# Storing the last block of a fused attention and two-MoE kernel in two halves, with the chunks of its last matmul rounds reordered around them

## The chip, the cores and the metric

The kernel runs on one core of a Trainium2 chip. The metric is the device time of one execution in microseconds (us), the median of three runs.

## The reference

The inputs are q, k and v of shape (4, 12, 448, 64): 4 batches of 448 tokens, 12 heads of 64 columns. Attention is without a softmax, with a sigmoid per score; its output, 1792 tokens by 768 columns, goes through two mixture-of-experts layers, each with 8 experts of which every token takes one.

```python
scores = scale * q @ k.T - log(S)
attn = sigmoid(scores) @ v
x = attn.transpose(0, 2, 1, 3).reshape(B * S, H * D)
# first layer: tokens with x @ w_skip > 0 only
e = argmax(x @ w_gate); gate = max of softmax(x @ w_gate)
x = x + gate * (relu(x @ w1[e]) @ w2[e])
# second layer: all tokens, cosine router
e = argmax(xn @ en.T / tau); gate = max of softmax
out = gate * (relu(x @ v1[e]) @ v2[e])
```

## The kernel before

The time falls into three stages. **Attention** takes pairs of heads in steps `g`; a step is `score` (PE, into a `psS` tile), a sigmoid on ACT, and two steps later `av` (PE, into `psO`). The operands of the first pairs are turned by PE transposes in `turn_first(nm, i)`, for nm "k" and "q" and for the halves i = 0 and 1: PE writes a bank `ps_t`, and four copies bring it into the tiles `kT` and `qT` (the call's j = 0 on DVE at L589, j = 1 on ACT at L587). The operands of later pairs arrive by DMA (`load_qk` on SP's queue, `load_v` on ACT's) and are turned by DVE at L593. Small setup steps are put between the steps `g`; one of them, `emb_turn` (L167 on PE), needs the expert embeddings scaled by GpSimd (POOL, L127), and that scaling stands on DVE behind the turn of the third pairs' q.

**Each MoE layer** is done block by block (a block is one batch of 448 tokens): most tokens of a block go to one expert, and `dense` computes the block with that expert's weights. The hidden columns are cut into NF = 8 chunks f. `h(f)` is 18 matmuls of 448 columns into one of the two banks (L785 to L787, "bank<-xs"); ACT (L805) and DVE (L806) turn it into the high part `hh` and the low part `hl`; `y(f)` is 18 matmuls, three for each of six feature chunks c, into the accumulators `YS[0..5]` ("y<-hh"). PE's order is h(0), h(1), y(0), h(2), y(1) and so on. `sub(k)` is called once after each h and once after each y, k = 0 to 15, and runs what a table of steps puts there: the splits of the next weights (L775 on ACT, L776 on DVE), loads, routing.

**The few tokens of other experts** are an `Item`. In the last block of the second layer its steps stand in the table of that block: `select` (DVE, slot 0), then by the three numbers given to `schedule` the steps `places` (four small matmuls L926 on PE into a bank, out by DVE at L929), `gather` (64 times: POOL reads a token's number and copies its column, L938, into the tile `stg`) and `gate`; at slots 13 and 15 `h(0)` and `h(1)` (24 matmuls each, L961), whose transposes are `hT` (L974, copied by DVE to `sel` at L975), and at the end `y` (32 matmuls L985). `put` multiplies on DVE (L999) and writes the rows by an indirect DMA from POOL (L1000); it waits for the block's own stores, onto whose rows it writes.

**The end of a block** is `finish`: the six accumulators are copied to `STG` (even c on ACT at L1308, odd c on DVE at L1306), transposed 24 times on PE (L1320), multiplied by the gate into `ROW` (ACT L1316, DVE L1314) and stored to `out`. For the last block the store is in two pieces: the feature blocks 0 to 3 on SP's queue and 4 and 5 on ACT's (L1335). An engine runs its instructions in program order, and so does each queue.

Of the kernel before, what the change touches and what calls it, by code (L numbers as in the profile page):

```python
# [10 lines left out]
F32 = mybir.dt.float32  # L11
F32R = mybir.dt.float32r
I32 = mybir.dt.int32
AF = mybir.ActivationFunctionType
# [7 lines left out]
def sigmoid_attention_moe_moe_kernel(  # L22
# [19 lines left out]
    P = 112  # L42
# [486 lines left out]
    def attention():  # L529


        with ExitStack() as a:
# [39 lines left out]
            def turn_first(nm, i):  # L572
                if i == 0:
                    ST[0, nm] = wk.tile([128, 2, S], F32, tag=nm + "T", name=nm + "T")
                ps = bank("ps_t")
                for j in range(2):
                    for e in range(2):
                        nc.tensor.transpose(
                            ps[:, (2 * j + e) * P : (2 * j + e + 1) * P],
                            LDU[0][nm][:, i, j, 2 * e * D : (2 * e + 2) * D], ident[:P, :P],  # L580
                        )
                for j in range(2):
                    for o in range(2):
                        src = ps[D * o : D * o + D, 2 * j * P : (2 * j + 2) * P].rearrange("r (e p) -> r p e", e=2)
                        dst = ST[0, nm][D * j : D * j + D, i].rearrange("r (p e o) -> r p e o", e=2, o=2)[:, :, :, o]
                        if j:
                            nc.scalar.activation(dst, src, AF.Copy)  # L587
                        else:
                            nc.vector.tensor_copy(dst, src)  # L589
# [198 lines left out]

    NF = 2 * NU

    def dense(xs, sub, f0=0, f1=NF):

        def h(f):
            h1, l1 = W[f // 2 % 2][:2]
            g = f % 2 * 128
            ps = bank("ps_h")
            for c in range(ND):
                mm3(  # L800
                    ps[:, :S], h1[:, c, g : g + 128], l1[:, c, g : g + 128], xs[:, 0, c, :], xs[:, 1, c, :],
                    c == 0, c == ND - 1,
                )
            a, l = HH[f % 2], HL[f % 2]
            nc.scalar.activation(a, ps[:, :S], AF.Relu)  # L805
            nc.vector.scalar_tensor_tensor(l, ps[:, :S], 0.0, a.bitcast(F32), op0=ALU.max, op1=ALU.subtract)  # L806

        def y(f):
            h2, l2 = W[f // 2 % 2][2:]
            g = f % 2  # L810
            for c in range(ND):
                mm3(
                    YS[c][:, :S], h2[:, g, c * 128 : c * 128 + 128], l2[:, g, c * 128 : c * 128 + 128],
                    HH[f % 2], HL[f % 2], f == 0, f == NF - 1,
                )

        for f in range(f0, f1):
            h(f)
            sub(2 * f)
            if f:  # L820
                y(f - 1)
            sub(2 * f + 1)
        if f1 == NF:
            y(NF - 1)
# [42 lines left out]
    class Item:  # L867
# [99 lines left out]

            return f

        def hT(self, s):  # L970
            def f():
                ps = bank("ps_ht")
                for i in range(2):
                    nc.tensor.transpose(ps[:, i * 128 : i * 128 + 128], self.hs[:, i * 128 : i * 128 + 128], ident)  # L974
                nc.vector.tensor_copy(SEL[:, s * 256 : s * 256 + 256], ps[:, :256])  # L975

            return f
# [320 lines left out]
    e = expert_of(0)  # L1298
    b = nc.values_load(K["pb"][0:1, 8:9], engines=[ENG.SP], min_val=0, max_val=B - 1)

    def finish(j, b, end=False):

        for c in range(ND):
            o = STG[:, c * S : (c + 1) * S]
            if c % 2:
                nc.vector.tensor_copy(o, YS[c][:, :S])  # L1306
            else:
                nc.scalar.activation(o, YS[c][:, :S], AF.Copy)  # L1308
        g = dense_gate(R2, j)

        def scaled(c, d, n, t):
            row = ROW[:P, c * DM + d * 128 : c * DM + (d + n) * 128]
            if (c + (n == 2)) % 2:
                nc.vector.tensor_scalar(row, t, g[:, c : c + 1], None, op0=ALU.mult)  # L1314
            else:
                nc.scalar.activation(row, t, AF.Copy, scale=g[:, c : c + 1])  # L1316

        def turn(t, w, c, d):
            o = d * S + c * P
            nc.tensor.transpose(t[:P, w : w + 128], STG[:, o : o + P], ident)  # L1320

        def tail():
            if end:
                banks = BANKS + YS[1:5]
                for d0, n, m in ((0, 4, 1), (4, 2, 2)):
                    place = [(banks[d0 + c // m], c % m * 256) for c in range(C)]
                    for d in range(d0, d0 + n):
                        for c, (t, w) in enumerate(place):
                            turn(t, w + (d - d0) * 128, c, d)
                    for c, (t, w) in enumerate(place):  # L1330
                        scaled(c, d0, n, t[:P, w : w + n * 128])
                    cols = slice(d0 * 128, (d0 + n) * 128)
                    queue, bq = (nc.sync, b) if d0 == 0 else (nc.scalar, batch_of(j))
                    to = out.rearrange("(b c p) d -> p b c d", c=C, p=P)[:, ds(bq, 1), :, cols]
                    STORES.append(queue.dma_start(  # L1335
                        to.rearrange("p o c d -> p (o c) d"),
                        ROW[:P].rearrange("p (c d) -> p c d", d=DM)[:, :, cols],
                    ))
                tc.declare_no_dep(STORES[1].ins, STORES[0].ins, reason="disjoint columns")
                return  # L1340
            at = 0
            for c in range(C):
                for d0, n in ((0, 4), (4, 2)):
                    t = YS[at % ND]
                    at += 1
                    for d in range(d0, d0 + n):
                        turn(t, (d - d0) * 128, c, d)
                    scaled(c, d0, n, t[:P, : n * 128])
            nc.sync.dma_start(
                out.rearrange("(b c p) d -> p b c d", c=C, p=P)[:, ds(b, 1)].rearrange("p o c d -> p (o c) d"),  # L1350
                ROW[:P].rearrange("p (c d) -> p c d", d=DM),
            )

        return tail

    pend, STORES = None, []
    for j in range(B):
        box = {"e": e}
        last = j == B - 1
        if last:  # L1360
            todo = {}
        else:
            steps = route2_steps(j + 1, XST[(j + 1) % 2])
            todo = at_subs((3, 5, 7, 1, 2, 2, 5, 6, 8, 9, 11), steps)
        if j == 0:
            load_unit(v1, v2, e, 1)
            halves()
            for f in split_unit(0, FIRST_RAW)[3:]:
                f()
            todo = merge({-0.5: lambda: spread(item_b())}, todo)  # L1370
        if j == B - 2:
            todo = merge(todo, item_steps(R2, (11, 13, 15)))
        if pend:
            todo = merge({-0.5: pend}, todo)

        def units2(k):
            u, r = k // 4, k % 4
            if r == 0 and u + 2 < NU:
                load_unit(v1, v2, box["e"], u + 2)
            if k == 10 and not last:  # L1380
                box["n"] = expert_of(j + 1)
                load_unit(v1, v2, box["n"], 0)
            if (u + 1 < NU or not last) and r % 2 == 0:
                for f in split_unit((u + 1) % NU)[:3] if r == 0 else split_unit((u + 1) % NU)[3:]:
                    f()
            if k == 12 and not last:
                load_unit(v1, v2, box["n"], 1)

        xs = XST[j % 2]
        if not last:  # L1390
            dense(xs, beside(units2, todo))
            pend = finish(j, b)
            b, e = nc.values_load(K["pb"][0:1, 9 + j : 10 + j], engines=[ENG.SP], min_val=0, max_val=B - 1), box["n"]
            continue
        with tc.If(count(R2) > 0) as cmp:  # L1395
            it = Item(1, 0)
            at, prep = it.ready(0)
            dense(xs, beside(units2, schedule(merge(todo, at), prep, (3, 3, 7))))
            it.hT(1)()
            finish(j, b, True)()  # L1400
            it.finish([None] * 3)
            info = mybir.DependencyInfo(mybir.DependencyClass.Sync, mybir.DependencyReason.DATA)
            tc.add_manual_dep(it.put().ins, STORES[0].ins.name, info, reason="the rows it lands on")
        with cmp.Else():
            STORES = []
            dense(xs, beside(units2, todo))
            finish(j, b, True)()
    more = nc.values_load(R2.LI[0:1, 3 * NL + 1 : 3 * NL + 2], min_val=0, max_val=NL)  # L1408
    with tc.If(more > 0):
        others(1)  # L1410
# [33 lines left out]
```

## Time and profile before

| | |
|---|---|
| median of 3 runs | 579.96 us (579.85 to 580.21) |
| the profiled execution: its own time | 579.14 us |
| its span, first to last instruction | 577.3 us |
| PE busy | 557.1 us, 96% |
| DVE, ACT, POOL busy | 302.1, 262.9, 45.3 us |
| mean granted TensorE clock | 0.994 |

The own time of the profiled execution is 1.84 us more than its span, and 0.82 us less than the median. All times of the trace are counted from the start of the span.

### The profile page before, as it was taken

The page shows a single profiled execution, that of the slowest core. Times are in us where ns is not written, and L with a number is a line of the kernel's source. Part 1 is how long each engine was busy: PE and PEld are TensorE (multiplying, and loading weights), DVE is VectorE, ACT ScalarE, POOL GpSimd, SP SyncE. Part 2 cuts the span into 40 slices and gives each one's busy share as a digit, 9 for nine tenths or more (in the row PEclk, how much of TensorE's full clock was granted, in tenths as well). Part 3 has the DMA queues.
Part 4 walks back from the last instruction along what each step waited for, and adds up shares of the span by engine and source line. Part 5 has one row for each costly group of instructions (what it writes and reads, how often), then busy time and mean ns, then how long its engine had stood idle before and what let it go on. Part 6 is the DMA issues. An engine that isn't in the chain of part 4 may idle for free. (4 is left out here: it accounts for less than half of the span.)

```text
span 577.3 us, 10262 instructions
## 1 busy us (share of the span) xinstructions
PE 557.1 (96%) x3719; PEld 434.1 (75%) x3719; DVE 302.1 (52%) x766; ACT 262.9 (46%) x429; POOL 45.3 (8%) x147
## 2 busy tenths in 40 slices
PE   8999999999999999999999999999999999899994
PEld 4554645544599988998778999979997999799871
DVE  2634434256957678561368653687347664533021
ACT  5766766767832363430156333933266332422021
POOL 4010000000000000651000000000000000055100
PEclk9999999999999999999999999999999999999997
DMA  9999786876342414235563060713227060653343
GB/s 148 146 134 121 120 123 109 129 100 203 118 150 70 152 36 146 97 111 185 202 223 110 0 219 0 250 66 124 97 74 241 0 219 1 198 173 109 95 180 103
DMA packets 138206, 73.37 MB, mean 127 GB/s; under 512 B 102066, under 2 KB 128006, under 8 KB 138128
## 3 DMA queue, kind: packets, MB, share of 16 engines
q1 hardware_dynamic: 116384, 65.94, 43.4%
q10 hardware_dynamic: 21360, 5.97, 5.6%
q0 software_dynamic: 384, 0.53, 0.6%
q8 instruction: 36, 0.59, 0.5%
q14 instruction: 42, 0.34, 0.2%
HBM read 66.90 MB, written 5.70 MB: 126 GB/s over the span
## 5 line engine op out<-in xcount | busy, mean ns | idle before, releaser
L805 ACT ACTIVATE hh<-bank 128x448 fp32r<-128x448 f32 x48 | 26.0, 542 | 192.0 <-PE bank L787 165.8
L785 PE MATMUL bank<-xs,h 128*128 128x448 f32 x288 | 107.4, 373 | 3.2 <-DVE hl L806 1.3
L785 PE MATMUL y<-hh,h 128*128 128x448 f32 x288 | 107.5, 373 | 0.0
L786 PE MATMUL y<-hl,h 128*128 128x448 f32 x288 | 105.6, 367 | 0.0
L787 PE MATMUL y<-hh,l 128*128 128x448 f32 x288 | 105.6, 367 | 0.0
L786 PE MATMUL bank<-xs,h 128*128 128x448 f32 x288 | 105.3, 366 | 0.0
L787 PE MATMUL bank<-xs,l 128*128 128x448 f32 x288 | 105.2, 365 | 0.1
L606 ACT ACTIVATE A<-psS,bias 128x896 f32<-128x896 f32 x84 | 83.3, 1006 | 35.6 <-PE psS L602 35.3
L806 DVE SCALAR_TENSOR_TENSOR hl<-bank,hh 128x448 fp32r<-128x448 f32 x48 | 29.9, 623 | 123.2 <-ACT hh L805 122.2
L776 DVE TENSOR_TENSOR l<-r,h 128x512 fp32r<-128x512 f32 (+1 forms) x115 | 85.4, 792 | 4.6 <-ACT h L775 3.0
L602 PE MATMUL psS<-qT,kT 64*64 64x448 f32 x672 | 87.3, 541 | 0.3 <-ACT A L606 0.3
L620 PE MATMUL psO<-A,v 64*64 64x448 f32 x672 | 86.3, 539 | 0.0
L775 ACT ACTIVATE h<-r 128x512 fp32r<-128x512 f32 (+1 forms) x115 | 74.6, 710 | 0.0
L785 PEld LDWEIGHTS bank<-xs,h 128*128 128x128 f32 x288 | 54.0, 187 | 12.1 <-DVE hl L806 2.7
L620 PEld LDWEIGHTS psO<-A,v 64*64 64x64 f32 x672 | 34.7, 133 | 32.2 <-issue 19.9
L785 PEld LDWEIGHTS y<-hh,h 128*128 128x128 f32 x288 | 54.1, 188 | 6.0 <-issue 1.0
L787 PEld LDWEIGHTS bank<-xs,l 128*128 128x128 f32 x288 | 54.0, 188 | 5.4 <-DVE l L776 0.4
L787 PEld LDWEIGHTS y<-hh,l 128*128 128x128 f32 x288 | 54.1, 188 | 5.0
L786 PEld LDWEIGHTS y<-hl,h 128*128 128x128 f32 x288 | 54.1, 188 | 4.8 <-issue 0.2
L786 PEld LDWEIGHTS bank<-xs,h 128*128 128x128 f32 x288 | 54.1, 188 | 4.3
L602 PEld LDWEIGHTS psS<-qT,kT 64*64 64x64 f32 x672 | 32.5, 132 | 30.4 <-issue 16.2
L527 DVE COPY xT<-psO 64x448 f32<-64x448 f32 x24 | 14.9, 622 | 43.1 <-PE psO L620 42.9
(251 smaller groups left out, 451.8 us busy)
## 6 DMA issues: line engine op xcount, KB each, us to landing
r<-in_moe_w_dram SPq DMA_DIRECT2D x62, 768.0 KB, 6.0
k<-in_k_dram SPq DMA_DIRECT2D x44, 112.0 KB, 3.6
q<-in_q_dram SPq DMA_DIRECT2D x44, 112.0 KB, 4.8
v<-in_v_dram ACTq DMA_DIRECT2D x44, 112.0 KB, 3.7
out_dram<-row SPq DMA_DIRECT2D x3, 1344.0 KB, 6.8
out_dram<-row SPq DMA_DIRECT2D x1, 896.0 KB, 5.4
stg<-in_moe_w_dram SPq DMA_DIRECT2D x1, 768.0 KB, 6.5
row<-in_moe_w_dram SPq DMA_DIRECT2D x1, 768.0 KB, 7.7
```

The source lines that it names most:

```text
L527: nc.vector.tensor_copy(x, ps[64 * j : 64 * j + 64, :S])
L602: nc.tensor.matmul(ps[KT * i : KT * i + KT, j, :S], lhsT=kT[r, i, h * KT : (h + 1) * KT], rhs=qT[r, i], start=True, stop=True,)
L606: nc.scalar.activation(at, ps[:, :, :S], AF.Sigmoid, bias=bias, scale=1.0 / math.sqrt(D))
L620: nc.tensor.matmul(ST[w, "o"][i][D * j : D * j + D, :S], lhsT=t[r, j, h, :], rhs=at[r, j, :], start=h == 0, stop=h == NH - 1,)
L775: nc.scalar.activation(dst_h, src, AF.Copy)
L776: nc.vector.tensor_sub(dst_l, src, dst_h.bitcast(F32))
L785: nc.tensor.matmul(ps, lhsT=ah, rhs=bh, start=first, stop=False)
L786: nc.tensor.matmul(ps, lhsT=ah, rhs=bl, start=False, stop=False)
L787: nc.tensor.matmul(ps, lhsT=al, rhs=bh, start=False, stop=last)
L805: nc.scalar.activation(a, ps[:, :S], AF.Relu)
L806: nc.vector.scalar_tensor_tensor(l, ps[:, :S], 0.0, a.bitcast(F32), op0=ALU.max, op1=ALU.subtract)
```

## The change

Three things change.

1. In `turn_first` all four copies of k are done by DVE and all four of q by ACT (before: j = 0 of both by DVE, j = 1 by ACT), and the half i = 1 is written to a `psO` tile instead of the two banks.
2. In the last block the three numbers for the item's steps are (5, 5, 7) instead of (3, 3, 7): `places` and `gather` move from the slot behind y(0) to the slot behind y(1).
3. `dense` ends otherwise in the last block. Its last two rounds of y go chunk by chunk, each chunk is copied to `STG` as soon as it is complete, the feature blocks 0 to 2 are transposed and stored after chunk 3, and 3 to 5 after chunk 5. The item's h(1) stands now after three chunks of y(6), and its `hT(1)` behind the last chunk, in `YS[0]` instead of a bank. The number of the batch for ACT's store is read ahead of the chunks.

```diff
-                ps = bank("ps_t")
+                ps = psO.tile([128, 512], F32, tag="psO", name="ps_t") if i else bank("ps_t")
...
-                        if j:
+                        if nm == "q":
                             nc.scalar.activation(dst, src, AF.Copy)
...
             h(f)
             sub(2 * f)
+            if end and f == NF - 1:
+                end(yc, lambda: sub(2 * f + 1))
+                return
...
+    def finish_last(j, b, it=None):
+        place = {0: BANKS + YS[1:3], 3: YS[3:5] + BANKS}
...
+        def store(g, d0, queue, bq):
+            for c, t in enumerate(place[d0]):
+                scaled(g, c, d0, 3, t[:P, : 3 * 128])
...
+        def end(yc, rest):
+            g = dense_gate(R2, j)
+            bq = batch_of(j)
+
+            def both(c):
+                yc(NF - 2, c)
+                yc(NF - 1, c)
+                copy(c)
+
+            for c in range(3):
+                yc(NF - 2, c)
+            rest()
+            for c in range(3):
+                yc(NF - 1, c)
+                copy(c)
+            both(3)
+            for d in range(3):
+                turns(d)
+            store(g, 0, nc.sync, b)
+            both(4)
+            both(5)
+            turns(3)
+            turns(4)
+            if it:
+                it.hT(1, YS[0])()
+            turns(5)
+            store(g, 3, nc.scalar, bq)
...
-            dense(xs, beside(units2, schedule(merge(todo, at), prep, (3, 3, 7))))
-            it.hT(1)()
-            finish(j, b, True)()
+            steps = schedule(merge(todo, at), prep, (5, 5, 7))
+            dense(xs, beside(units2, steps), end=finish_last(j, b, it))
             it.finish([None] * 3)
```

The changed kernel's lines are some lower down: L1314 and L1316 become L1310 and L1312, L1306 and L1308 become L1352 and L1354, L929 becomes L935, L975 becomes L981.

At the very start of the program, ACT's rows before, from its first load to the first sigmoids:

```order
L544 DMA q_128<-in_q_dram 112x2x256 x2
L632 ACT_TABLE_LOAD
L632 ACTIVATE bias<-bias 128x1
L587 ACTIVATE kT<-ps_t 64x224 x2
L587 ACTIVATE qT<-ps_t 64x224 x2
L587 ACTIVATE kT<-ps_t 64x224 x2
L587 ACTIVATE qT<-ps_t 64x224 x2
L606 ACTIVATE A<-psS,bias 128x896 x3
```

and of the change:

```order
L544 DMA q_128<-in_q_dram 112x2x256 x2
L632 ACT_TABLE_LOAD
L632 ACTIVATE bias<-bias 128x1
L587 ACTIVATE qT<-ps_t 64x224 x8
L606 ACTIVATE A<-psS,bias 128x896 x3
```

ACT has eight copies in both; kT has left ACT, and on DVE qT has left in the same way.

In the last block, DVE's rows before, from the last step of `select` (sel) on. hl is the low part that L806 makes of an h, l are the weights' low parts, and L929 is the way out of `places`:

```order
L911 TENSOR_SCALAR sel<-io,small 112x128 x4
L806 SCALAR_TENSOR_TENSOR hl_78<-bank_1721,hh_76 128x448
L776 TENSOR_TENSOR l_1735<-r_92,h_1734 128x768 x2
L929 TENSOR_SCALAR stg<-bank_1721 1x64
L806 SCALAR_TENSOR_TENSOR hl_77<-bank_1720,hh_75 128x448
L776 TENSOR_TENSOR l_1729<-r_89,h_1728 128x512 x3
L806 SCALAR_TENSOR_TENSOR hl_78<-bank_1721,hh_76 128x448
```

and of the change:

```order
L917 TENSOR_SCALAR sel<-io,small 112x128 x4
L806 SCALAR_TENSOR_TENSOR hl_78<-bank_1721,hh_76 128x448
L776 TENSOR_TENSOR l_1735<-r_92,h_1734 128x768 x2
L806 SCALAR_TENSOR_TENSOR hl_77<-bank_1720,hh_75 128x448
L776 TENSOR_TENSOR l_1729<-r_89,h_1728 128x512 x3
L935 TENSOR_SCALAR stg<-bank_1720 1x64
L806 SCALAR_TENSOR_TENSOR hl_78<-bank_1721,hh_76 128x448
```

The way out of `places` stands one round later, behind the hl of h(2) and three splits, and its bank is that of h(2) (bank_1720) instead of that of h(1) (bank_1721).

At the end of the last block, DVE's rows before, from the copies of the two `hT` (sel; the first of them runs a round earlier) to `put`; y_1722 to y_1727 are the accumulators of the chunks 0 to 5 and later hold transposes, dg is the gate:

```order
L975 COPY sel<-bank_1720 128x256 x2
L1306 COPY stg<-y_1723 128x448
L1306 COPY stg<-y_1725 128x448
L1306 COPY stg<-y_1727 128x448
L347 TENSOR_TENSOR dgt<-OH_106,PRIM_110 112x32
L350 TENSOR_REDUCE dg<-dgt 112x4
L351 TENSOR_TENSOR dg<-dg,gr_363 112x4
L1314 TENSOR_SCALAR row<-bank_1721,dg 112x512
L1314 TENSOR_SCALAR row<-y_1724,dg 112x512
L1314 TENSOR_SCALAR row<-y_1725,dg 112x256
L1314 TENSOR_SCALAR row<-y_1726,dg 112x256
L999 TENSOR_SCALAR xg_73<-y_1722,small 128x384
```

and of the change (the rows of the gate, which now stand at the head, left out, as is `small` ahead of the last):

```order
L1352 COPY stg<-y_1723 128x448
L1352 COPY stg<-y_1725 128x448
L1310 TENSOR_SCALAR row<-bank_1721,dg 112x384
L1310 TENSOR_SCALAR row<-y_1724,dg 112x384
L1352 COPY stg<-y_1727 128x448
L981 COPY sel<-y_1722 128x256
L1310 TENSOR_SCALAR row<-y_1726,dg 112x384
L1310 TENSOR_SCALAR row<-bank_1721,dg 112x384
...
L1005 TENSOR_SCALAR xg_73<-y_1722,small 128x384
```

The copies of the accumulators stood behind the copy of `hT(1)` and now stand ahead of it, and half of the multiplications stands between them.

## Rows read from the trace of the kernel before

**Rows 1.** What POOL's queue ran for put, by line L1000; last columns first and last start.

```profile
L1000 POOLq EVENT_SEMAPHORE  x3: 43/43/43, 571.0 to 571.1; - x3
```

**Rows 2.** Timeline at the end: start us, us, engine, line, what [idle before <-releaser].

```profile
559.13 0.36 PE L787 MATMUL y<-hh,l 128*128 128x448 f32 x1
...
560.10 1.68 DVE L1306 COPY stg<-y 128x448 f32<-128x448 f32 x3
...
562.12 1.25 PE L1320 MATMUL y<-ident,stg 128*112 128x128 f32 x10
...
562.39 0.69 ACT L1316 ACTIVATE row<-bank,dg 112x512 f32<-112x512 f32 x1 [2.92 <-PE y L1320]
...
563.31 5.38 PE L985 MATMUL y<-r,sel 128*64 128x384 f32 x32
...
564.35 0.86 ACT L1316 ACTIVATE row<-y,dg 112x256 f32<-112x256 f32 x2 [0.69 <-DVE row L1314]
...
565.67 0.38 ACTq L1335 DMA_DIRECT2D out_dram<-row  x1
...
568.74 0.62 DVE L999 TENSOR_SCALAR xg<-y,small 128x384 f32<-128x384 f32 x1 [3.96 <-PE y L985]
```

**Rows 3.** DMA issues from 555 us on: KB each, us from issue to landing.

```profile
out_dram<-row SPq DMA_DIRECT2D x1, 896.0 KB, 5.4
out_dram<-row ACTq DMA_DIRECT2D x1, 448.0 KB, 5.3
```

**Rows 4.** Waits of PE in the last block: us in total, times, longest.

```profile
PE bank L926 <- DVE hl L806: 2.2, 1, 2.2
```

**Rows 5.** Timeline of PE in the last block, from y(0) to h(3).

```profile
501.41 0.37 PE L787 MATMUL y<-hh,l 128*128 128x448 f32 x1
503.96 0.61 PE L926 MATMUL bank<-sel,small 112*1 112x64 f32 x8 [2.18 <-DVE hl L806]
504.50 0.47 PE L785 MATMUL bank<-xs,h 128*128 128x448 f32 x1
...
511.91 0.37 PE L785 MATMUL bank<-xs,h 128*128 128x448 f32 x1
```

**Rows 6.** Timeline of DVE, POOL and PE, from hl to the item's h(0).

```profile
503.29 0.62 DVE L806 SCALAR_TENSOR_TENSOR hl<-bank,hh 128x448 fp32r<-128x448 f32 x1
...
505.56 0.20 DVE L929 TENSOR_SCALAR stg<-bank 1x64 int32<-1x64 f32 x1
...
506.37 0.20 POOL L938 COPY stg<-xT 128x6 f32 x1 [244.44 <-PE bank L787]
...
536.42 0.19 POOL L938 COPY stg<-xT 128x6 f32 x1 [0.27 <-issue]
...
542.38 2.81 PE L961 MATMUL bank<-r,stg 128*64 128x256 f32 x24
```

**Rows 7.** Timeline of DVE and POOL, one of four places where splits meet the gather.

```profile
517.14 1.83 DVE L776 TENSOR_TENSOR l<-r,h 128x768 fp32r<-128x768 f32 x2
...
517.36 2.07 POOL L938 COPY stg<-xT 128x6 f32 x5 [0.27 <-issue]
```

**Rows 8.** Timeline of the start, the copies of the first operands.

```profile
5.13 0.79 DVE L589 COPY kT<-ps_t 64x224 f32<-64x224 f32 x2 [1.80 <-PE ps_t L578]
...
6.02 0.73 ACT L587 ACTIVATE kT<-ps_t 64x224 f32<-64x224 f32 x2 [2.81 <-DVE kT L589]
...
6.80 0.60 PE L578 MATMUL ps_t<-ident,k 112*128 112x112 f32 x4 [0.78 <-ACT kT L587]
...
9.15 0.74 ACT L587 ACTIVATE qT<-ps_t 64x224 f32<-64x224 f32 x2
```

**Rows 9.** Timeline of DVE and PE, the turn ahead of the embeddings, and PE's wait for them.

```profile
28.18 1.11 DVE L593 STREAM_TRANSPOSE qT<-q 128x896 f32<-128x896 f32 x1 [1.31 <-DMA q<-in_q_dram]
...
32.95 0.53 PE L167 MATMUL ps_emb<-ident,emb 8*128 8x8 f32 x6 [0.77 <-POOL emb L127]
```

**Rows 10.** Windows: width, busy us of the engines, granted clock, DMA share, GB/s.

```profile
16.00:18.00 2.00, 2.00 (x28) 0.88 (x24) 0.70 (x1) 1.24 (x2) 0.00 (x0) 1.00 1.42 152
```

More of the change, by code (lines that the diff above doesn't have):

```diff
@@ L789, in sigmoid_attention_moe_moe_kernel, with dense @@
     NF = 2 * NU
-    def dense(xs, sub, f0=0, f1=NF):
+    def dense(xs, sub, f0=0, f1=NF, end=None):
         def h(f):
@@ L806, in h, with yc, y @@
             nc.vector.scalar_tensor_tensor(l, ps[:, :S], 0.0, a.bitcast(F32), op0=ALU.max, op1=ALU.subtract)
-        def y(f):
+        def yc(f, c):
             h2, l2 = W[f // 2 % 2][2:]
             g = f % 2
+            mm3(
+                YS[c][:, :S], h2[:, g, c * 128 : c * 128 + 128], l2[:, g, c * 128 : c * 128 + 128],
+                HH[f % 2], HL[f % 2], f == 0, f == NF - 1,
+            )
+        def y(f):
             for c in range(ND):
[L812 to L815, printed above, removed]
+                yc(f, c)
         for f in range(f0, f1):
@@ L968, in h, with hT @@
             return f
-        def hT(self, s):
+        def hT(self, s, at=None):
             def f():
-                ps = bank("ps_ht")
+                ps = bank("ps_ht") if at is None else at
                 for i in range(2):
@@ L1299, in sigmoid_attention_moe_moe_kernel, with scaled, turn_out, finish @@
     b = nc.values_load(K["pb"][0:1, 8:9], engines=[ENG.SP], min_val=0, max_val=B - 1)
-    def finish(j, b, end=False):
+    def scaled(g, c, d, n, t):
+        row = ROW[:P, c * DM + d * 128 : c * DM + (d + n) * 128]
+        if (c + (n == 2)) % 2:
+            nc.vector.tensor_scalar(row, t, g[:, c : c + 1], None, op0=ALU.mult)
+        else:
+            nc.scalar.activation(row, t, AF.Copy, scale=g[:, c : c + 1])
+    def turn_out(t, w, c, d):
+        o = d * S + c * P
+        nc.tensor.transpose(t[:P, w : w + 128], STG[:, o : o + P], ident)
+    def finish(j, b):
         for c in range(ND):
@@ L1309, in finish @@
         g = dense_gate(R2, j)
[L1311 to L1320, printed above, removed]
-        def tail():
[L1323 to L1340, printed above, removed]
+        def tail():
             at = 0
@@ L1346, in tail @@
                     for d in range(d0, d0 + n):
-                        turn(t, (d - d0) * 128, c, d)
-                    scaled(c, d0, n, t[:P, : n * 128])
+                        turn_out(t, (d - d0) * 128, c, d)
+                    scaled(g, c, d0, n, t[:P, : n * 128])
             nc.sync.dma_start(
@@ L1354, in finish, with copy, turns @@
         return tail
+    def finish_last(j, b, it=None):
+        place = {0: BANKS + YS[1:3], 3: YS[3:5] + BANKS}
+        def copy(c):
+            o = STG[:, c * S : (c + 1) * S]
+            if c % 2:
+                nc.vector.tensor_copy(o, YS[c][:, :S])
+            else:
+                nc.scalar.activation(o, YS[c][:, :S], AF.Copy)
+        def turns(d):
+            d0 = d // 3 * 3
+            for c, t in enumerate(place[d0]):
+                turn_out(t, (d - d0) * 128, c, d)
+        def store(g, d0, queue, bq):
+            for c, t in enumerate(place[d0]):
+                scaled(g, c, d0, 3, t[:P, : 3 * 128])
+            cols = slice(d0 * 128, (d0 + 3) * 128)
+            to = out.rearrange("(b c p) d -> p b c d", c=C, p=P)[:, ds(bq, 1), :, cols]
+            STORES.append(queue.dma_start(
+                to.rearrange("p o c d -> p (o c) d"),
+                ROW[:P].rearrange("p (c d) -> p c d", d=DM)[:, :, cols],
+            ))
+        def end(yc, rest):
[23 more added lines that the diff above has]
+            store(g, 3, nc.scalar, bq)
+            tc.declare_no_dep(STORES[1].ins, STORES[0].ins, reason="disjoint columns")
+        return end
     pend, STORES = None, []
@@ L1405, in sigmoid_attention_moe_moe_kernel @@
             STORES = []
-            dense(xs, beside(units2, todo))
-            finish(j, b, True)()
+            dense(xs, beside(units2, todo), end=finish_last(j, b))
     more = nc.values_load(R2.LI[0:1, 3 * NL + 1 : 3 * NL + 2], min_val=0, max_val=NL)
```

## The prediction, on record before the changed kernel ran

> **What bounds the kernel now.** PE runs nearly without a gap, so a change counts where it takes a gap of PE away or shortens what comes after PE's last matmul. I read the end first, backwards. The last work is `put`: POOL's semaphore waits for it pass at 571.0 to 571.1 [rows 1], and what follows to the end of the span at 577.3 does not change, 6.2 us. What releases it is the later of two things: the rows to be written, which DVE has at 568.74 + 0.62 = 569.4, and the landing of ACT's store, issued at 565.67 [rows 2] and under way for 5.3 us [rows 3], so 571.0. The store is last by 1.6 us. The reader is to see why it is issued so late: y ends on PE at 559.1, but DVE's three copies of the odd chunks run only from 560.10 to 561.78, and the eight multiplications follow behind the transposes, ACT's last pair ending at 565.2 [rows 2].
>
> Then I asked the waits for PE's own gaps in the last block. The one large row is `places`: 2.2 us [rows 4], between the last y(0) at 501.41 and the first h(2) at 504.50 [rows 5]. Its bank is that of h(1), whose hl runs on DVE only at 503.29, behind `select` [rows 6]. Third, the start: the eight copies run as a chain in which ACT waits 2.81 us for DVE, and PE waits for ACT before the second half [rows 8].
>
> **The end: 1.7 us, between 1.0 and 2.3.** I keep the clock of before and add the other terms afterwards. PE's work is the same, in another order. Ahead of the end of y stand 12 of the 24 transposes; ten take 1.19 us from 562.12 to the next matmul at 563.31 [rows 2], 0.12 each, so 1.4 us, and 0.3 for two changes between kinds of matmul (the first matmul behind a small group runs some 0.1 us longer, 0.47 against 0.37 [rows 5]). The last y so starts at 559.13 + 1.7 = 560.8. Behind it come 14 transposes, those of `hT(1)` among them, 1.7 us: to 562.5. The copy of chunk 5 (0.56 us, a third of the 1.68) is covered by the ten that don't need it. The first store lies wholly beside the y of chunks 4 and 5: its multiplications and its 672 KB cost nothing unless a bank is late; 12 matmuls of y, 2.5 us (36 take 7.41, [rows 5]), cover the two multiplications of each engine.
>
> For the second half each of ACT and DVE multiplies twice. Its width of 384 does not occur; 256 takes 0.43 and 512 takes 0.69 [rows 2], so 0.56. DVE has the copy of `hT(1)` ahead of it, under way while PE makes the last transposes. Two times 0.56 behind the last transposes at about 562.7 is 563.8, and the issue 563.9 instead of 565.67: 1.7 us earlier, since reading the batch number no longer stands in between. The landing I leave at 5.3 us: 448 and 896 KB together took 5.3 and 5.4 [rows 3], and 672 KB, now nearly alone, can't be much slower; 569.3 instead of 571.0. The other branch: the item's y starts at 562.6 instead of 563.31 and takes 5.38, DVE's rows are ready at 568.7. If the landing is faster than 4.7 us, this decides, and 571.0 - 568.7 = 2.3 is the most that the end can give. If the bank of a transposed chunk or a copy is late by one copy (0.56), 1.0 is left. What moves with it: h(1) of the item runs nine matmuls earlier, so SP issues the last two weight loads earlier; the read of the batch number stands on SP ahead of these, where SP waits for PE anyway, and on ACT in an idle stretch.
>
> **`places` a round later: 1.6 us, between 0.8 and 2.3.** Without the wait h(2) follows y(0) at 501.41 + 0.21 = 501.62 instead of 504.50, 2.88 us earlier. hl of h(1), ready at 503.9, is wanted only by y(1), at 505.3. Behind y(1), 7.41 us later [rows 5], comes `places`, at 509.0; its bank is free (that of h(2), whose readers are done two microseconds before), and it costs 504.50 - 503.96 = 0.54 us. So h(3) and all that follows moves up by 2.3 us. But the gather starts later. From L926 to POOL's first copy were 2.41 us before, 1.0 of it (503.96 + 0.61 to 505.56) because DVE was busy; behind y(1) DVE is through its splits (hl of h(2), by an estimate done at 506.7, then three narrower ones, at most 2.75 by the 1.83 for two in [rows 7]), so 1.4 remain: the gather starts at 510.4 instead of 506.37. It lasts 536.61 - 506.37 = 30.24 us [rows 6], so to 540.7. PE before wanted it at 542.38 and had it 5.8 us early; it will want it at 540.1 and get it at 540.75. So a new wait of some 0.65 us takes the place of the old: net 542.38 - 540.75 = 1.6. If the gather starts at once or runs faster, 2.3; if it starts 0.8 later, 0.8. Queued behind PE's new wait are h(7) and y; nobody else waits.
>
> The pace of the gather could change, since it now lies beside three groups of DVE's weight splits instead of four. In the trace a split of 1.83 us stretches POOL's copies beside it (five in 2.07 us, [rows 7]). But a copy of 0.19 and a wait of 0.27 for the next number make 0.46, and over the whole gather the pace is 30.05 / 63 = 0.477 [rows 6]: the four groups together cost at most 1.1 us, one of them 0.27, so the gather ends 0 to 0.3 us sooner; I leave it at 30.24.
>
> The Trainium skill (SBUF — State Buffer, section "Who interferes with whom") says that a DVE instruction with two SBUF inputs shuts out a GpSimd instruction that reads SBUF fully until it is done. By that rule one group less would shorten the gather by 1.83 us, PE would find it finished, and this term would be 2.3. The trace's pace beside the splits speaks for less.
>
> **The start: 0.3 us, between -0.4 and 1.0.** ACT's last copy ends at 9.15 + 0.74 = 9.9. In the change neither engine waits for the other: the second half is transposed at the latest at 6.80, as before, and at the earliest at 6.02, since PE stood free for 0.78 ahead of it; its q is one group behind (0.60), the copies begin when that group is done (0.60), and four of 0.37 follow on ACT [rows 8]: done at 8.7 to 9.5. The first step comes 0.4 to 1.2 us earlier; I take 1.0. What is late next: PE waits 0.77 us at 32.95 for the embeddings, whose last steps on DVE stand behind a turn at 28.18 that waited 1.31 us for a load of q [rows 9]. That load doesn't come from PE's order; the DMA queues are full in this stretch, share 1.42 [rows 10]. So PE would only wait longer there. Something may get through, as SP's loads wait in part for the v loads, which ACT issues behind its sigmoids and so earlier; but v loads that start earlier also share the engines with q. I take 0.3; -0.4 if they slow q by half a load (112 KB at the 152 GB/s in the window [rows 10] are 0.75 us), 1.0 if all gets through.
>
> **The sum.** 1.7 + 1.6 + 0.3 = 3.6 us. The profiled execution takes 579.14, so 575.5; the median of the runs lies 0.82 above it, so the forecast is 579.96 - 3.6 = 576.4.
>
> **Rivals.** (a) The gather is no bound, since it starts or runs faster: the second term is 2.3, 575.7. For it: only 0.65 us decide. (b) The start passes through to the end: 575.7; against it the full queues. Both together 575.0. (c) The end gives nothing, because PE stalls between the pieces: with banks and accumulators reused at once, three stalls of a copy's 0.56 eat the 1.7: 578.1. For it: chunk 5's copy and three readers of the same banks in a row; against it the covers above. (d) Slower: the gather comes much too late. Its list leaves DVE behind the splits of the next weights, and these wait for their load. If that read-out came 5 us late, at 514.7 instead of 509.7, the gather would end at 545.7, 3.3 us after the slot of before, and with the 2.0 of the other terms the kernel would be at 581.3; from 4.8 us on it is measurably slower. Against it: of the waits of DVE in the last block none was for a load. (e) The change does not do what it says, because something other than the rows named releases `put`; then 1.9 from the first two PE terms is left: 578.1.
>
> **Chances.** The forecast's case (all three terms near their values) 0.5; (a) 0.17, (b) 0.08, (c) 0.12, (d) 0.04, (e) 0.09. A measurement of this kernel can tell 0.2%, 1.2 us, from no change. Faster by more: all of the first three and most of (c) and (e), 0.9; within 0.2%: the worst of (c) and (e) with a start at -0.4, 0.06; slower 0.04. Range: from both gains together, a little beyond (b), at 574.8, to (c) and (e) at 578.1.
>
> **What would show it.** Right: no wait at `places`, POOL's first gather copy 0.8 us behind the read-out, a wait of PE before the item's h(0) of 0.3 to 1 us for POOL; a wait at the embeddings of more than 1 us; both stores issued, the second 3.4 to 3.8 us earlier than before, `put` released by its landing. Wrong: h(0) without a wait (a), the first wait at the embeddings unchanged with an earlier start (b), gaps of PE between the y of chunks 3, 4 and 5 (c). The forecast falls if the second store lands later than 5.6 us after its issue or the gather lasts over 31 us.

## The result, and the profile after

The changed kernel takes 574.86 us (median of 9 runs, 573.81 to 578.27) where the kernel before takes 580.07 in the same rounds (median of 9): the ratio is 0.992, 95% interval 0.9899 to 0.9941, so 3.4 to 5.9 us faster. Forecast were 576.4 us and 3.6 us, with a range of 574.8 to 578.1; the measured time lies at its lower edge. The profiled execution took 574.43 us, with a span of 572.6.

The end first, in the order of the prediction: what POOL's queue ran for `put`, by line, as in [rows 1].

```profile
L1006 POOLq EVENT_SEMAPHORE  x3: 43/43/699, 565.1 to 565.3; - x3
```

The third wait took 0.7 us where all took 0.04 before, and passed at 566.0. The timeline of the end shows with what, and answers to [rows 2]:

```profile
555.56 0.58 ACT L1312 ACTIVATE row<-bank,dg 112x384 f32<-112x384 f32 x1 [1.65 <-PE bank L1316]
...
557.00 0.36 SPq L1366 DMA_DIRECT2D out_dram<-row  x1
...
557.92 0.37 PE L787 MATMUL y<-hh,l 128*128 128x448 f32 x1
...
559.42 0.42 DVE L981 COPY sel<-y 128x256 f32<-128x256 f32 x1 [0.40 <-PE y L980]
...
559.90 0.20 PEld L991 LDWEIGHTS y<-r,sel 128*64 128x64 f32 x4 [0.33 <-DVE sel L981]
559.90 5.38 PE L991 MATMUL y<-r,sel 128*64 128x384 f32 x32
...
561.04 0.38 ACTq L1366 DMA_DIRECT2D out_dram<-row  x1
565.35 0.62 DVE L1005 TENSOR_SCALAR xg<-y,small 128x384 f32<-128x384 f32 x1 [4.39 <-PE y L991]
566.88 1.09 POOL L1006 DMA_INDIRECT out_dram<-xg,small  x1 [27.19 <-DVEq L1453]
```

DVE's rows are ready at 565.35 + 0.62 = 565.97, and that is the third wait. The second store had landed by then, 4.1 us after its issue at 561.04, as the list of DMA issues (KB each, us to landing) shows beside [rows 3]:

```profile
out_dram<-row SPq DMA_DIRECT2D x1, 672.0 KB, 4.2
out_dram<-row ACTq DMA_DIRECT2D x1, 672.0 KB, 4.1
```

In the last block the only wait of PE above 0.5 us is a new one, for the gather; [rows 4] had 2.2 us at `places`. The rows below are that of the waits and then, from the timeline, those that answer to [rows 5, 6].

```profile
PE bank L967 <- POOL stg L944: 0.6, 1, 0.6
```

```profile
500.31 0.36 PE L787 MATMUL y<-hh,l 128*128 128x448 f32 x1
...
507.99 0.61 PE L932 MATMUL bank<-sel,small 112*1 112x64 f32 x8
...
508.63 0.21 DVE L935 TENSOR_SCALAR stg<-bank 1x64 int32<-1x64 f32 x1 [1.19 <-PE bank L932]
...
509.45 0.20 POOL L944 COPY stg<-xT 128x6 f32 x1 [248.21 <-DVE stg L935]
...
539.50 0.20 POOL L944 COPY stg<-xT 128x6 f32 x1 [0.27 <-issue]
...
539.74 2.88 PE L967 MATMUL bank<-r,stg 128*64 128x256 f32 x24 [0.58 <-POOL stg L944]
```

And the start, against [rows 8, 9]:

```profile
6.30 3.17 ACT L587 ACTIVATE qT<-ps_t 64x224 f32<-64x224 f32 x8 [3.10 <-PE ps_t L578]
...
27.72 1.11 DVE L593 STREAM_TRANSPOSE qT<-q 128x896 f32<-128x896 f32 x1 [1.27 <-DMA q<-in_q_dram]
...
32.50 0.54 PE L167 MATMUL ps_emb<-ident,emb 8*128 8x8 f32 x6 [0.73 <-POOL emb L127]
```

ACT now copies without a gap from 6.30 to 9.47, and PE's wait at the embeddings is as long as before and 0.45 us earlier. Read by itself this says that the start passes through. One more gap differs: behind the item of the first layer PE waits 0.21 us where the trace of before has 0.85, though no work there was touched.

### The profile page after: what moved, and what is told of

Same layout as the page of the kernel before. It is cut to its first block, busy times and chain, and to the rows that moved or that the text cites. A ratio compares the mean times of both kernels' runs of the same rounds, so it can differ in the third digit from the quotient of the medians.

```text
span 572.6 us, 10258 instructions
## 1 busy us (share of the span) xinstructions
PE 557.4 (97%) x3719; PEld 435.8 (76%) x3719; DVE 302.4 (53%) x766; ACT 263.1 (46%) x429; POOL 43.9 (8%) x147
## 4 chain that ended last, share of the span: by engine, by line
PE 79%; issue 5%; DVE 4%; ACT 3%; DMA 3%; POOLq 3%; POOL 1%; DVEq 0%; ACTq 0%
PE psS L602 9%; PE y L785 9%; PE bank L785 9%; PE y L787 9%; PE y L786 9%; PE psO L620 8%; PE bank L786 8%; PE bank L787 8%; POOLq L942 2%; PE bank L967 2%; PE y L991 2%; PE y L1316 2%; DMA out_dram<-row 1%; DMA v<-in_v_dram 1%; ACT A L606 1%
## 5 line engine op out<-in xcount | busy, mean ns | idle before, releaser
L806 DVE SCALAR_TENSOR_TENSOR hl<-bank,hh 128x448 fp32r<-128x448 f32 x48 | 29.9, 623 | 120.1 <-ACT hh L805 119.0
```

## The experiments

A table holds all profiled executions, cut where the parts of the change meet: when PE starts the last y(0) matmul, from there to the item's h(0), from h(0) to `put`, and from `put` to the end of the span. The second and the third column change only with the code, but for 0.13 us; the last moves without it too, between 5.2 and 5.8 us.

| kernel | y(0) | to h(0) | to put | to the end |
|---|---|---|---|---|
| before | 501.41 | 40.97 | 29.66 | 5.3 |
| changed | 500.31 | 39.43 | 27.14 | 5.7 |
| 1 start only | 502.19 | 41.00 | 29.67 | 5.4 |
| 2 places only | 500.35 | 39.46 | 29.79 | 5.2 |
| 3 end only | 500.49 | 41.05 | 27.03 | 5.5 |
| 4 places early | 501.29 | 38.74 | 27.02 | 5.4 |
| 5 with the old start | 500.95 | 38.73 | 27.03 | 5.5 |
| 6 v later | 500.43 | 38.73 | 27.03 | 5.6 |
| 7 half of the item's y | 499.49 | 39.45 | 26.81 | 5.5 |
| 8 first store held | 501.00 | 39.47 | 27.11 | 5.5 |
| 9 both stores at once | 504.18 | 39.46 | 28.41 | 5.3 |
| 10 best | 500.42 | 38.73 | 26.52 | 5.8 |
| 11 new division alone | 500.47 | 39.43 | 27.13 | 5.6 |
| 12 psO alone | 502.08 | 39.45 | 27.09 | 5.7 |

**1 to 3: each part alone**, on the kernel before (the parts of the diff in the section on the change).

> The kernel before with the first part of the change alone (all copies of k on DVE, all of q on ACT, the second half in a psO tile). Theory A (the start passes through): the first step comes 0.4 to 1.0 us earlier, the turn of the third pairs' q moves up with it, the wait of PE for the embeddings stays at 0.7 to 0.8 us, and the kernel gains the same 0.4 to 1.0 us. Theory B (the prediction's: the load of q holds the turn): that wait grows to more than 1 us and the kernel gains at most 0.3 us. PE's wait of 0.85 us behind the item of the first layer (at 293 us) stays as it was before in both, as no work there is touched; if it is 0.2 us here too, the step of 0.64 us seen there in the changed kernel belongs to no part of the change.

Measured: 580.38 us, ratio to before 1.0017 (1.0000 to 1.0034): nothing gained. The first sigmoid started at 10.5 instead of 10.9 us, but the second pair's q came late: the timeline shows DVE waiting 4.64 us to turn it (at 17.30 before; the wait is put down to a load of k on the same queue), and PE 1.89 us behind that (put down to the next instruction of DVE).

```profile
20.08 1.11 DVE L593 STREAM_TRANSPOSE qT<-q 128x896 f32<-128x896 f32 x1 [4.64 <-DMA k<-in_k_dram]
...
21.33 0.98 PE L602 MATMUL psS<-qT,kT 64*64 64x448 f32 x8 [1.89 <-DVE io L131]
```

So theory B in kind, a pair earlier than it said. The wait behind the first layer's item was 0.59 here and between 0.2 and 1.1 in the other runs: it belongs to no part.

> The kernel before with the second part alone (places and gather a slot later). Theory A: no wait at places, the gather starts 3.0 us later and lasts 30.2 us, PE waits 0.5 to 0.7 us for it before the item's h(0), and everything behind comes 1.5 us earlier; the kernel gains 1.5 us. Theory B (the trace of the changed kernel owes this part more, since the other parts moved the weight splits): h(0) comes 2 us earlier or more. Theory C: DVE's read-out comes later without the other parts; under 1 us gained.

Measured: 576.81 us, ratio 0.9946 (0.9925 to 0.9967). In the trace from y(0) to h(0) it is 40.97 - 39.46 = 1.51 us, with a wait of 0.59 for the gather: theory A. The time gained more, 3.4 us by the medians, 1.9 to 4.4 by the interval; in the profiles the first column holds 1.06 us of it, and the rest of it is taken up below, under what the sum left out.

> The kernel before with the third part alone (the last block's end chunk by chunk, stores of three and three feature blocks, hT(1) behind the last chunk). Theory A: the second store is issued 2.0 to 2.4 us earlier against the item's h(0) and lands within 4.3 us, put is released by DVE's rows, 0.7 to 1.0 us behind that landing, and the kernel gains 2.0 to 2.5 us. Theory B (the prediction's middle): the store's landing takes 5.3 us and releases put; 1.7 us gained. Theory C: much of the changed kernel's gain at the end came from elsewhere; under 1 us gained.

Measured: 577.51 us, ratio 0.9955 (0.9939 to 0.9971); 29.66 - 27.03 = 2.63 us between h(0) and `put`. The stores landed in 4.1 to 4.2 us and the third wait of `put` was for the rows: theory A, a little beyond its upper end.

**4: places earlier.**

```diff
-            turn[0] ^= 1
+            turn[0] ^= self.m == 0
...
-            steps = schedule(merge(todo, at), prep, (5, 5, 7))
+            steps = schedule(merge(todo, at), prep, (3.5, 3.5, 7))
```

> The changed kernel with places directly behind h(2), in the bank of h(1), which is free there, and its read-out on DVE directly behind hl of h(2), ahead of the next weight split. Theory A: the gather starts some 3 us earlier than in the changed kernel (at 506.5 instead of 509.5), lasts 30.2 us again although one more group of splits lies beside it, and is done 2 us before PE wants it; the wait of 0.58 us before h(0) is gone and the kernel is 0.6 us faster than the changed kernel, so 573.9 to 574.3 where that takes 574.6. Theory B (a split with two SBUF inputs shuts POOL out while it lasts): the gather lasts 1.8 us longer, 32.1 us, and still is done in time. Theory C: the read-out or places waits, and h(0) waits as before; no gain.

Measured: 574.26 us, ratio 0.9900 (0.9877 to 0.9923). From y(0) to h(0) 0.7 us less than in the changed kernel, no wait there. The splits on DVE and the gather, from the timeline of this kernel, the first and the last copy with the four places where they meet:

```profile
506.69 1.87 DVE L776 TENSOR_TENSOR l<-r,h 128x512 fp32r<-128x512 f32 x3
...
507.37 1.63 POOL L944 COPY stg<-xT 128x6 f32 x4 [245.60 <-DVE l L776]
...
515.10 2.07 POOL L944 COPY stg<-xT 128x6 f32 x5 [0.28 <-issue]
...
523.06 2.07 POOL L944 COPY stg<-xT 128x6 f32 x5 [0.27 <-issue]
...
530.56 2.09 POOL L944 COPY stg<-xT 128x6 f32 x5 [0.27 <-issue]
...
537.42 0.20 POOL L944 COPY stg<-xT 128x6 f32 x1 [0.28 <-issue]
```

With four groups of splits beside it the gather takes 537.62 - 507.37 = 30.25 us; in the changed kernel, with three, 539.70 - 509.45 = 30.25. So neither the 1.8 us of theory B nor the 0.27 us that the prediction gave a group is there. But single copies are held. The first row gives the shortest, the median and the longest of the 64 copies in ns; the other two, from the timeline, are the second split of the group at 514.75 and the second copy of the run at 515.10:

```profile
L944 POOL COPY stg<-xT x64: 189/194/1254, 507.4 to 537.4; 128x6 f32 x64
```

```profile
515.63 0.95 DVE L776 TENSOR_TENSOR l<-r,h 128x768 fp32r<-128x768 f32 x1
515.70 0.93 POOL L944 COPY stg<-xT 128x6 f32 x1
```

That copy takes 0.93 us instead of 0.19 and ends at 516.63, 0.05 us behind the split. In all the traces every copy that starts inside a split, more than 0.15 us before its end, ends 0.05 to 0.06 us behind the end of one. Meanwhile POOL's queue goes on reading the next numbers every 0.47 us (at 515.09, 515.56, 516.03, 516.49 and 516.97), and the copies behind a held one follow closer, here 0.13 and 0.28 us apart. So the run of five, with the 0.28 us ahead of it, takes 2.35 us, five times 0.47. Theory B is right that a split shuts POOL out, and wrong on what this costs the gather.

**5 and 6: the start taken apart**, both on the kernel of 4. In 5 `turn_first` is that of before; in 6 ACT's v loads of the second pair come a step later.

```diff
-                ps = psO.tile([128, 512], F32, tag="psO", name="ps_t") if i else bank("ps_t")
+                ps = bank("ps_t")
...
-                        if nm == "q":
+                        if j:
```

```diff
-                if w + 1 < N and 0 <= h - LAG < 4:
-                    load_v(w + 1, h - LAG)
+                if w + 1 < N and 0 <= h - LAG - (w == 0) < 4:
+                    load_v(w + 1, h - LAG - (w == 0))
```

> The kernel of the fourth experiment (places early) with the start of before, so the second and third part of the change without the first. Theory A (the new start gives nothing, since its earlier v loads delay the second pair's q, which DVE then turns at 17.9 to 20.1 us instead of 17.2 to 17.4): the turn is back at 17.2 to 17.4, no wait of PE for it at 20 to 21 us, and the kernel is as fast as the fourth experiment or up to 1.2 us faster, 573.1 to 574.3. Theory B (the first step coming 0.4 to 1.0 us earlier is worth what it saves): 0.4 to 1.0 us slower than the fourth experiment, 574.7 to 575.3.

Measured: 574.02 us, ratio 0.9887 (0.9870 to 0.9904), q turned at 16.96, no wait of PE. As fast as 4 without the new start: theory A as to the time. The cause that it names is what 6 tests.

> The kernel of the fourth experiment (with the new start), in which ACT issues the four loads of the second pair's v one step later. Theory A (these loads, issued from 12.5 us instead of 13.1 to 13.7, share the DMA engines with the second pair's q and make it late): with the first of them at 13.4 us or later the turn of q is back at 17.2 to 17.5, PE's wait of 1.1 to 1.9 us at 20 to 21 us is gone, and the kernel gains up to 1 us against the fourth experiment, unless v itself comes late. Theory B (q's landing has nothing to do with the v loads): the turn stays between 17.9 and 20.1.

Measured: 573.88 us, ratio 0.9886 (0.9868 to 0.9904); the first v load was issued at 13.31, and q was still turned only at 18.61, with 0.6 us of PE's waiting (before, it was issued at 13.06 and q turned at 17.30). Theory A, that it is these loads, is not borne out.

**7: half of the item's y.**

```diff
-                            start=s + g + i == 0, stop=s + g + i == 3,
+                            start=s + g + i == 0, stop=s + g + i == (3 if self.m == 0 else 2),
...
-                self.y(s)
+                if s == 0 or self.m == 0:
+                    self.y(s)
```

> The changed kernel in which the item's y leaves out the second half of the hidden columns, 16 of its 32 matmuls: DVE's rows are ready 2.7 us earlier and nothing else changes. Theory A (put waits for the later of the rows and the second store's landing, and in the changed kernel the rows are last by 0.8 us): put is released by the landing, 4.1 to 4.2 us behind the second store's issue, and goes 0.7 to 0.9 us earlier against that issue than in the changed kernel. Theory B (something else, the order of the branch at the block's end, say, releases it): put moves by the whole 2.7 us or not at all.

Measured: 572.97 us (one run). The rows were ready at 562.55, 2.6 us earlier against y(0), and `put` went at 565.75: its waits passed at 564.7 to 564.8, when the second store, issued at 560.20, had landed after 4.5 us. From the timeline:

```profile
560.20 0.38 ACTq L1367 DMA_DIRECT2D out_dram<-row  x1
...
561.93 0.62 DVE L1005 TENSOR_SCALAR xg<-y,small 128x384 f32<-128x384 f32 x1 [1.82 <-PE y L991]
565.75 1.09 POOL L1006 DMA_INDIRECT out_dram<-xg,small  x1 [26.87 <-SPq L1454]
```

So `put` waits for the later of the two, and the rows are last in the changed kernel, by 0.8 us (565.97 against 565.1). `put` gained 0.3 us of this, as the store landed 0.4 later here.

**8 and 9: both stores together.** 8 issued the first store behind the last multiplication in program order; 9 also exchanged the queues:

```diff
-            store(g, 0, nc.sync, b)
+            scale3(g, 0)
...
-            store(g, 3, nc.scalar, bq)
+            scale3(g, 3)
+            store(g, 0, nc.scalar, bq)
+            store(g, 3, nc.sync, b)
```

(`scale3` holds the multiplications that `store` began with.)

> The changed kernel with the first store held back, so that both stores of 672 KB are issued together behind the last multiplication. Theory A (a store lands in 4.1 us because it is alone; the 5.3 us of before came from two stores on the way together, 1344 KB in the 7.0 us from the first issue to the second landing): the landings take 6 to 7 us and put goes 1.5 to 2 us later against the second issue. Theory B (the 5.3 us belonged to the sizes or the pieces of 1 KB and 2 KB rows): both land in 4.1 to 4.5 us and put is where it was.

Measured: 574.94 us (one run), and no answer: SP has nothing else to do there and issued the store at 557.71, as soon as its data were ready. Writing it later doesn't hold it back.

> The changed kernel with the first store issued by ACT behind its last multiplication and the second by SP, so that both stores of 672 KB are on the way at once. Theory A (a store lands in 4.1 us when it is alone; 5.3 us in the kernel before came from two on the way together, 1344 KB in the 7.0 us from the first issue to the second landing): landings of 6 to 7 us, put released by a landing, 1 to 2 us later against the issue at the multiplications' end than in the changed kernel. Theory B (the time belongs to the size or the shape of the pieces): landings of 4.1 to 4.5 us and put released by DVE's rows as in the changed kernel.

Measured: 579.16 us (one run). Of this, 3.9 us against the changed kernel are lost before y(0): q was turned only at 20.00, PE waited 2.40 us until 21.25, and behind that wait the granted clock was 0.50 (1.2 GHz) for a while, and 1.00 again from 26 us on. The window from 22 to 24 us:

```profile
22.00:24.00 2.00, 2.00 (x16) 0.84 (x12) 1.71 (x16) 0.86 (x1) 0.00 (x0) 0.50 0.71 107
```

The issues, from the timeline, and the landings, from the list of DMA issues:

```profile
563.86 0.38 ACTq L1368 DMA_DIRECT2D out_dram<-row  x1
...
564.90 0.36 SPq L1368 DMA_DIRECT2D out_dram<-row  x1
...
572.05 1.10 POOL L1006 DMA_INDIRECT out_dram<-xg,small  x1 [28.46 <-SPq L1457]
```

```profile
out_dram<-row ACTq DMA_DIRECT2D x1, 672.0 KB, 4.6
out_dram<-row SPq DMA_DIRECT2D x1, 672.0 KB, 6.0
```

From the first issue to the last landing 564.90 + 6.0 - 563.86 = 7.0 us, as in the kernel before (565.67 + 5.3 - 564.05, SP's issue there, = 6.9). A landing releases `put` again, 1.3 us later against h(0) than in the changed kernel. Theory A, though of the two landings only the second took the 6 to 7 us that it says.

**10: two more edits at the end, on the kernel of 5.**

```diff
-                it.hT(1, YS[0])()
+                it.hT(1, YS[1])()
...
-            nc.vector.tensor_scalar(yg, YS[0][:, :hw], GS[:, 0:1], None, op0=ALU.mult)
+            nc.vector.tensor_scalar(yg[:, : hw // 2], YS[0][:, : hw // 2], GS[:, 0:1], None, op0=ALU.mult)
+            nc.scalar.activation(yg[:, hw // 2 :], YS[0][:, hw // 2 : hw], AF.Copy, scale=GS[:, 0:1])
```

> The fifth experiment (places early, the start of before) with two small edits at the end: hT(1) is transposed into YS[1], which is free, instead of YS[0], which the item's y writes, and the rows of put are multiplied by DVE and ACT together, half the columns each. Theory A (put hangs on PE's y and then on the rows): the wait of 0.33 us before the item's y is gone and the rows take 0.4 instead of 0.62 us, so put goes 0.4 to 0.5 us earlier against the last y of the block; 573.4 to 573.8 where the fifth takes 574.0. Theory B (the second store's landing comes next at once): at most 0.2 us.

Measured: 573.78 us (572.97 to 573.99), ratio 0.9889 (0.9874 to 0.9905): faster than the kernel before. It is 1.1 us below the changed one by the medians of different rounds, whose intervals against before overlap; from y(0) to `put` its trace is 1.3 us shorter. `put` goes 65.76 - 65.25 = 0.51 us earlier against y(0) than in 5, the size of theory A but not by its way, as the timeline of this kernel shows:

```profile
559.05 5.38 PE L991 MATMUL y<-r,sel 128*64 128x384 f32 x32
...
564.51 0.42 DVE L1005 TENSOR_SCALAR xg<-y,small 128x192 f32<-128x192 f32 x1 [4.18 <-PE y L991]
564.96 0.42 ACT L1006 ACTIVATE xg<-y,small 128x192 f32<-128x192 f32 x1 [5.08 <-DVE xg L1005]
565.67 1.10 POOL L1007 DMA_INDIRECT out_dram<-xg,small  x1 [28.92 <-ACT xg L1006]
```

y starts 0.15 us earlier against y(0); the two halves run one after the other, so the rows take 0.87 us; but `put` follows 0.29 us behind them, where it stood 0.9 behind DVE's in 5 and in the changed kernel. What POOL's queue ran for it, by line, says more:

```profile
L1007 POOLq EVENT_SEMAPHORE  x3: 17/43/43, 564.6 to 564.7; - x3
```

These three waits were through at 564.74, when the second store had landed (issued at 560.41, 4.1 us) and before the rows were done at 565.38: the wait for ACT's half is that of the DMA itself. In the other 13 profiles `put` starts 0.86 to 0.87 us behind the last of the three (571.18 to 572.04 before, 566.01 to 566.88 in the changed kernel), here 0.93. So this stretch, whose work isn't known, now runs beside the second half instead of behind the rows. And the landing, which theory B names, is next: by these rows still faster ones would gain an estimated 0.06 us (565.67 - 564.74 - 0.87).

**11 and 12: the two edits of the start alone**, each beside the second and third part: 11 leaves out the psO tile (the first line that the diff in 5 changes), 12 the new division of the copies (the second).

> The changed kernel whose start has the new division of the copies (k on DVE, q on ACT) but writes the second half to the two banks as before. If the earlier first step makes the second pair's q late, the turn of q on DVE comes at 17.6 us or later when the first sigmoid starts before 11 us, and at 17.4 or earlier when it starts at 11.3 or later. If one edit has its own effect on the load, the turn tells which, together with the next run.

> The changed kernel whose start has the second half in psO tiles but the old division of the copies (j = 0 on DVE, j = 1 on ACT). Expected as for the run before it: the turn of the second pair's q at 17.6 us or later goes with a first sigmoid before 11 us, if the earlier first step is what makes it late.

Measured: 574.38 and 576.11 us (one run each). The new division alone, with a first sigmoid at 11.24, had q at 17.01; psO alone, at 10.39, had it at 17.72, and DVE then waited 1.92 us for the third pair's q, PE 1.38 at the embeddings. Over all profiles: in the seven whose first sigmoid starts by 10.52 q is turned at 17.67 to 20.08, in six of the other seven at 16.96 to 17.74, and in 8, with 10.87, at 18.96. Divided by the psO tile, the eight profiles with it have q at 17.67 to 20.08 and the six without it at 16.96 to 17.74, and 8 is no exception. No kernel without the tile had its first sigmoid before 10.94, so these runs don't tell an early first step from the tile; 8 (10.87, q at 18.96) beside 10 (10.94, 17.74) speaks for the tile.

## Why the prediction held

**Places: right, term by term.** 1.6 forecast, 1.5 measured alone and in the whole. h(2) follows y(0) without a wait; the gather starts 509.45 - 500.31 = 9.1 us behind y(0) (forecast 9.0), lasts 30.25 (30.24), and PE waits 0.58 (0.65). Rivals (a) and (d) fall with it. The 1.83 us that the prediction worked out by the page's rule for one group less are not there: 4 against the changed kernel shows 0.00. The Trainium skill (SBUF — State Buffer, "Who interferes with whom") says that a DVE instruction with two SBUF inputs contends with a GpSimd instruction that reads SBUF, and that the lock is exclusive. The traces agree: a copy that starts inside a split ends only behind it, after 0.93 us instead of 0.19 in 4. What failed is the step from this hold to a longer gather. The gather goes at the pace at which the numbers are read, 0.47 us, and the copies behind a held one make up for it.

**The end: right mechanism, the landing mis-sized.** Forecast 1.7, measured 2.5 to 2.6, more than the 2.3 that the prediction called the most. PE did as worked out: against h(0) the last y starts 1.4 us later (1.7) and the item's y 0.8 earlier (0.7). The second store is issued 2.0 us earlier (1.7). The step that failed is "the landing I leave at 5.3 us": nearly alone a store of 672 KB lands in 4.1 (4.5 in 7), and the 5.3 of before came from two on the way, of which 9 shows another pair. So the other branch that the prediction named, the rows at 2.3, decided, and its sign that `put` is released by the landing did not come. Most of the 0.2 beyond it is POOL's: the landing at 571.0 was followed by three waits up to 571.18, the rows at 565.97 by the end of one at 566.01. Rivals (c) and (e) fall: no gap stands between the pieces, and 7 beside the changed kernel shows both releasers.

**The start: right to count it near nothing, wrong on where it is lost.** Forecast 0.3 with a growing wait at the embeddings. That wait did not grow in the profile of the changed kernel, and its 0.45 us looked like rival (b); 1 and 5 show no gain that belongs to the start. The second pair's q comes late, by up to 2.8 us; a longer wait for the third's stands in 12 alone (1.92 us against 1.31), where the wait at the embeddings grew to 1.38. Over the kernels the new start is worth nothing, or a small loss. What makes q late isn't settled: the early first step or the psO tile; the v loads were moved without effect.

**What the sum left out.** The two parts give 1.5 + 2.5 = 4.0 us; the medians say 5.2, the ratio 4.6 (3.4 to 5.9), so the rest isn't clear of the noise. The time lies inside the range by 0.06 us, and the sum had neither the faster landing nor this rest in it. In the two profiles, 577.3 - 572.6 = 4.7 us apart, the rest is in the first column: 1.1 us up to y(0), of it 0.64 in the gap behind the first layer's item, with 0.5 us taken back behind `put`. That column lies between 499.49 and 504.18 over these kernels, and 2 and 3, whose work up to y(0) is that of before, stand at 500.4. Why before is late there in its profile isn't settled.

The clock in executions without a trace can be a part of it. For 36 of the kernel before the mean granted clock is on record: the 24 at 0.990 to 0.993 have a median of 580.4 us, the 12 at 0.994 to 0.997 one of 579.5. The profiled one has 0.994, and its clock is below 1.00 only behind PE's last matmul (0.50 from 571 us on). Of the changed kernel's nine, eight have 0.996 or more, and all six of 2, which gained more than its trace shows, 0.995 or more. This would fit a clock that falls in many executions of before where PE waits, as in 9. It isn't shown: no trace of before has such a fall, and the end alone moves the mean (0.997 in the profile of 1, where the clock fell 4 us later at the end).

## What to carry to other kernels

Where the end waits for the later of a store's landing and a last computation, take the landing time of a store from one with nothing beside it if the change spreads the stores out, and cost both branches. A gain ahead of a stretch that is fed by full DMA queues is worth what the loads allow: test it alone before it is added to a sum. A hold on single instructions costs a chain only where they set its pace: look at the starts of the next ones before giving it a price. And cut the traces at instructions where the parts meet: the two middle segments repeated to 0.13 us between kernels with the same code there, while the time up to y(0) scattered by 4.7.

## What the runs showed that was not expected

Two stores together took 7.0 us for 1344 KB however they were cut (896 and 448, or 672 twice), one of 672 KB nearly alone 4.1 to 4.5. DVE's splits hold POOL's copies to their end, up to 1.26 us long, and the gather takes 30.23 to 30.27 us all the same, in all fourteen traces. The first transposes of the program ran at 0.61 us for four in the trace of before and 1.01 in that of the changed kernel, with a granted clock of 1.00 (2.4 GHz) recorded in both and 14 transposes of the identity ahead of them in both. The first sigmoid came 0.4 us earlier than before there, and 1.0 in experiment 9, where they took 0.60.
